# Turning q and the attention scores by transposing DMAs instead of on TensorE, in a fused attention and gated-FFN kernel

## The chip, the cores and the metric

The kernel runs on one core of one Trainium2 chip. The metric is the device time of one execution in microseconds (us). Executions of one kernel mostly agree within a few tenths of a per cent, so differences of 1% are readable with a handful of runs. The variants ran in several rounds, on different chips, each time with the kernel before beside them (medians 623.2 to 624.1 us): a ratio is within one round, a difference of two times from different rounds is good to about 1 us. The profiles are of single executions and give a span about 2 us shorter than the time of that execution.

## The reference, cut to what matters

Eight batches of 1024 tokens, eight heads of 64. Keys and values are first projected along the sequence from 1024 to 64 rows, so the scores are only 64 wide per head. The attention output, 8192 tokens by 512, goes through a gated feed-forward network (FFN).

```python
k_proj = np.einsum('ks,bhsd->bhkd', E, k)          # 64 x 64 per head
v_proj = np.einsum('ks,bhsd->bhkd', F, v)
scores = scale * np.matmul(q, k_proj.transpose(0, 1, 3, 2))
attn = softmax(scores)                             # over 64
attn_out = np.matmul(attn, v_proj)
# x: (8192, 512)
g = x @ w_gate                                     # 512 -> 1536
out = (g * sigmoid(g) * (x @ w_val)) @ w_out       # 1536 -> 512
```

The matmuls of this kernel contract over partitions. q arrives with tokens on partitions and must be turned so that the head dimension is there; the normalised scores must be turned once more before they meet the projected values.

## The kernel before: the parts that matter

Each batch is worked in eight steps j of 128 tokens, four to a half batch (ch). These are the two turns, both on TensorE, each with a copy from PSUM to SBUF:

```python
def u_T(b, j):                                     # turn q
    ps = ps_a.tile([P, NPAIR, P], BF16, name="qTp", tag="pa")
    src = qb[b, j // 4]
    for pr in range(NPAIR):                        # NPAIR = 4
        nc.tensor.transpose(out=ps[:, pr, :], in_=..., identity=ident_bf[:])
    t = aw.tile([P, NPAIR, P], BF16, name="qT", tag="qT")
    nc.scalar.copy(out=t[:], in_=ps[:])
    qT[b, j] = t

def u_A(b, j):                                     # turn the normalised scores
    ...                                            # four transposes into aTp
    nc.vector.tensor_copy(out=AT[b, ch][:, :, j % 4, :], in_=ps[:])
```

Between them stand `u_S` (score matmuls and the exponential on ACT), `u_R` (sum and reciprocal on DVE) and `u_N` (normalisation on POOL). `u_PV` multiplies the turned scores with the projected values and writes the FFN's input xT. `u_KV` projects k and v.

The FFN of one batch is 24 steps of 12 matmuls, and the attention of the next batch is dealt into its gaps, in 48 "slots" per batch, two to a step. The first half of batch 0 has no FFN to hide in and stands alone ahead of the loop:

```python
        load_k(0, 4); load_q(0, 0); load_v(0, 2)   # written on three lines
        ...                                        # weights, casts, load_q(0, 1)
        load_k(1)
        load_v(1)
        load_q(1, 0)
        load_q(1, 1)
        ...
        u_KV(0, 0, 8)
        u_KT(0)
        for n in range(7):                         # u_T, u_S, u_R, u_N, u_A of steps 0 to 3, pipelined
            ...
        for pr in range(NPAIR):
            u_PV(0, 0, pr)
```

The loads of k and v are issued from POOL and convert to bf16 on the way; the loads of q and the output stores are issued from SyncE (SP). Each of these two engines issues in program order: in the timeline before, SyncE's fourth q load goes out at 27.6 us, when its buffer is free, and nothing written after it goes out earlier.

The softmax here doesn't subtract the row's maximum and nothing guards it: scores larger than these inputs give would overflow.

Of the kernel before, what the change touches and what calls it, by code (L numbers as in the profile page):

```python
# [12 lines left out]
BF16 = mybir.dt.bfloat16  # L13
FP32 = mybir.dt.float32

B = 8
H = 8
S = 1024
D = 64
KP = 64  # L20
DM = H * D
DFF = 1536
P = 128
NJ = S // P
NPAIR = H // 2
NKT = DM // P
NFT = DFF // P
CH = 2
CW = 512
# [4 lines left out]
def kernel(  # L34
# [19 lines left out]
    nc = tc.nc  # L54
# [7 lines left out]
    aw = ctx.enter_context(tc.tile_pool(name="aw", bufs=2))  # L62
# [7 lines left out]
    ps_a = ctx.enter_context(tc.tile_pool(name="psa", bufs=3, space=bass.MemoryType.PSUM))  # L70

    ident_bf = const.tile([P, P], BF16, name="ident_bf")
# [4 lines left out]
    BD = [const.tile([P, NPAIR, P], BF16, name=f"BD{i}") for i in range(2)]  # L77
# [8 lines left out]
    kb, vb, qr, qb, xT, hT = {}, {}, {}, {}, {}, {}  # L86
# [85 lines left out]

    qT, ee, rr, AA, AT = {}, {}, {}, {}, {}

    def u_T(b, j):
        ps = ps_a.tile([P, NPAIR, P], BF16, name="qTp", tag="pa")
        src = qb[b, j // 4]
        for pr in range(NPAIR):
            nc.tensor.transpose(  # L179
                out=ps[:, pr, :], in_=src[:, j % 4, 2 * pr : 2 * pr + 2, :].rearrange('p h d -> p (h d)'), identity=ident_bf[:]  # L180
            )
        t = aw.tile([P, NPAIR, P], BF16, name="qT", tag="qT")
        nc.scalar.copy(out=t[:], in_=ps[:])  # L183
        qT[b, j] = t

    def u_S(b, j):
        ps = ps_a.tile([P, NPAIR, P], FP32, name="sc", tag="pa")
        t = qT.pop((b, j))
        for pr in range(NPAIR):
            nc.tensor.matmul(  # L190
                out=ps[:, pr, :], lhsT=t[:, pr, :], rhs=BD[b % 2][:, pr, :], start=True, stop=True
            )
        e = aw.tile([P, H, KP], FP32, name="ee", tag="ee", bufs=3)
        nc.scalar.activation(  # L194
            out=e[:].rearrange("p h k -> p (h k)"),
            in_=ps[:].rearrange("p a k -> p (a k)"),
            func=AF.Exp,
            scale=scale,
        )
        ee[b, j] = e  # L200

    def u_R(b, j):
        e = ee[b, j]
        z = aw.tile([P, H], FP32, name="zz", tag="zz", bufs=3)
        nc.vector.reduce_sum(out=z[:], in_=e[:], axis=AX.X)  # L205
        r = aw.tile([P, H], FP32, name="rr", tag="rr", bufs=3)
        nc.vector.reciprocal(out=r[:], in_=z[:])  # L207
        rr[b, j] = r

    def u_N(b, j):  # L210
        a = aw.tile([P, H, KP], BF16, name="AA", tag="AA", bufs=3)
        nc.gpsimd.tensor_tensor(  # L212
            out=a[:],
            in0=ee.pop((b, j))[:],
            in1=rr.pop((b, j))[:].unsqueeze(2).to_broadcast([P, H, KP]),
            op=ALU.mult,
        )
        AA[b, j] = a

    def u_A(b, j):  # L220
        ch = j // 4
        if (b, ch) not in AT:
            AT[b, ch] = aw.tile([P, NPAIR, 4, P], BF16, name="AT", tag="AT")
        ps = ps_a.tile([P, NPAIR, P], BF16, name="aTp", tag="pa")
        a = AA.pop((b, j))
        for pr in range(NPAIR):
            nc.tensor.transpose(  # L227
                out=ps[:, pr, :], in_=a[:, 2 * pr : 2 * pr + 2, :].rearrange('p h d -> p (h d)'), identity=ident_bf[:]
            )
        nc.vector.tensor_copy(out=AT[b, ch][:, :, j % 4, :], in_=ps[:])  # L230

    def u_PV(b, ch, pr):
        if (b, ch) not in xT:
            xT[b, ch] = x_pool.tile([P, NPAIR, CW], BF16, name="xT", tag=f"xT{ch}")
        ps = ps_a.tile([P, CW], FP32, name="pv", tag="pa")
        nc.tensor.matmul(  # L236
            out=ps[:],
            lhsT=BDV[b % 2][:, pr, :],
            rhs=AT[b, ch][:, pr].rearrange("p j t -> p (j t)"),
            start=True,  # L240
            stop=True,
        )
        nc.scalar.copy(out=xT[b, ch][:, pr, :], in_=ps[:])  # L243


    gp = {}
# [60 lines left out]
    slots = defaultdict(list)  # L307

    def put(s, fn, *a):
        slots[s].append((fn, a))  # L310

    def place(b):
        s0 = 48 * (b - 1)
        if b == 1:
            ks, tb, step = 28, 32, 2
        else:
            ks, tb, step = 0, 8, 5
        for i in range(4):
            put(s0 + ks + (i if b > 1 else i // 2), u_KV, b, i, 2)
        put(s0 + ks + (6 if b > 1 else 3), u_KT, b)  # L320
        for j in range(NJ):
            t = s0 + tb + step * j
            put(t, u_T, b, j)
            put(t + 2, u_S, b, j)
            put(t + 3, u_R, b, j)
            put(t + 3, u_N, b, j)
            put(t + 7, u_A, b, j)
        for ch in range(CH):
            if b == 1:
                at = (s0 + 48 - 2, s0 + 48 - 2, s0 + 48 - 1, s0 + 48 - 1) if ch == 0 else (  # L330
                    s0 + 57, s0 + 59, s0 + 62, s0 + 64)
            else:
                at = (36, 39, 41, 44) if ch == 0 else (57, 59, 62, 64)
                at = tuple(s0 + a for a in at)
            for pr in range(NPAIR):
                put(at[pr], u_PV, b, ch, pr)

    def run_slot(s):
        for fn, a in slots.pop(s, ()):
# [2 lines left out]
    with tc.manual_schedule():  # L342

        ef = []
        for which, src in (("E", E), ("F", F)):
            raw = const.tile([KP, S], FP32, name=f"{which}raw")
            nc.sync.dma_start(out=raw[:], in_=src)
            ef.append(raw)
        load_k(0, 4)
        load_q(0, 0)  # L350
        load_v(0, 2)
        for i in range(2):
            nc.vector.memset(BD[i][:], 0.0)
            nc.vector.memset(BDV[i][:], 0.0)
        load_w_gv(0)
        cast_q(0, 0)
        load_q(0, 1)
        load_w_gv(1)
        load_w_gv(2)
        load_wo(0)  # L360
        load_wo(1)
        cast_q(0, 1)
# [4 lines that stand above are left out]
        for which in range(2):  # L367
            for half in range(2):
                ps = ps_a.tile([P, 4, KP], FP32, name="efp", tag="pa")
                for i in range(4):  # L370
                    j = 4 * half + i
                    nc.tensor.transpose(
                        out=ps[:, i, :],
                        in_=ef[which][:, bass.ds(j, P, step=NJ)],
                        identity=ident_fp[:KP, :KP],
                    )
                js = slice(4 * half, 4 * half + 4)
                if which == 0:
                    nc.vector.tensor_copy(out=ET[:, js, :], in_=ps[:])
                else:  # L380
                    nc.scalar.copy(out=FT[:, js, :], in_=ps[:])

        u_KV(0, 0, 8)
        u_KT(0)
        for n in range(7):
            if n < 4:
                u_T(0, n)
            if 1 <= n < 5:
                u_S(0, n - 1)
                u_R(0, n - 1)  # L390
                u_N(0, n - 1)
            if n >= 3:
                u_A(0, n - 3)
        for pr in range(NPAIR):
            u_PV(0, 0, pr)
        for j in range(4, NJ):
            t = 3 * (j - 4)
            put(t, u_T, 0, j)
            put(t + 2, u_S, 0, j)
            put(t + 3, u_R, 0, j)  # L400
            put(t + 3, u_N, 0, j)
            put(t + 7, u_A, 0, j)
        for pr in range(NPAIR):
            put(19 + pr, u_PV, 0, 1, pr)
        for b in range(1, B):
            place(b)
        for b in range(2, B):
            s0 = 48 * (b - 2)
            put(s0 + 36, load_k, b)
            put(s0 + 40, load_v, b)  # L410
            put(s0 + 36, load_q, b, 0)
            put(s0 + 44, load_q, b, 1)
        for b in range(1, B):
            s0 = 48 * (b - 1)
            put(s0 + 1 if b > 1 else 27, cast_q, b, 0)
            put(s0 + 20 if b > 1 else 35, cast_q, b, 1)

        for s in slots:
            slots[s].sort(key=lambda x: x[0] not in (load_k, load_v, load_q, cast_q))

        for t in range(NIT):
            c, f = divmod(t, NFT)
            f_g(c, f)
            run_slot(2 * t)
            f_v(c, f)
            if c > 0:
                f_y(c - 1, f)
            run_slot(2 * t + 1)
        for f in range(NFT):
            f_y(B * CH - 1, f)  # L430
        assert not slots
# [30 lines left out]
```

## Time and profile before

| | before |
|---|---|
| time, median of 4 runs | 623.83 us |
| span of the profiled execution (it took 625.48 us) | 623.7 us |
| PE busy | 587.5 us (94%) |
| first gate matmul of the FFN (L252) | 41.67 us |
| steady batch | 72.2 us, PE busy for all of it |
| PE's waits for DMAs | 4.4 (E), 9.2 (first k), 8.7 (v: 8.1 first, 0.6 batch 2) |

The table has two messages. PE is full from 42 us on, so anything taken off PE there shortens the run by as much. Up to 42 us PE mostly waits, first for loads and then for a chain of small steps. The lines behind it are in the prediction below, with their reading.

```profile
out_dram<-ysb SPq DMA_DIRECT2D x1, 256.0 KB, 6.2
```

### The profile page before, as it was taken

What the parts mean: (1) busy time and instruction counts of PE and PEld (TensorE: products, weight loads), DVE (VectorE), ACT (ScalarE), POOL (GpSimd) and SP (SyncE); (2) the same over time, 40 slices, a digit from 0 to 9 for tenths busy, and PEclk for the clock granted to TensorE, in tenths of its full rate; (3) what the DMA queues carried; (4) which work ended last, traced back from release to release, by engine and by line L of the source; (5) the groups of instructions that cost most, each with busy time, mean ns of one, the idle gap of its engine ahead of it and who ended that gap; (6) DMA issues with size and microseconds to landing.
All of it is one profiled execution on the core that took longest, in us unless ns stands there. A gap on an engine that the chain in (4) does not pass through costs nothing.

```text
span 623.7 us, 8720 instructions
## 1 busy us (share of the span) xinstructions
PE 587.5 (94%) x3312; PEld 283.3 (45%) x3312; DVE 352.2 (56%) x614; ACT 258.9 (42%) x459; POOL 126.6 (20%) x164
## 2 busy tenths in 40 slices
PE   1369999999999999999999999999999999999996
PEld 1135455445544455444544545445553455444442
DVE  1049566566655665556655566555665666655540
ACT  1145446254444445344452544344353444433321
POOL 4634013221220311203220212202112121100000
PEclk9959999999999999999999999999999999999999
DMA  9999049000770019200490008600192000000001
GB/s 194 244 229 205 6 114 222 20 35 18 148 190 23 29 34 221 101 34 35 70 251 35 35 35 159 162 34 18 44 243 85 18 35 35 34 35 33 36 34 68
DMA packets 47498, 56.14 MB, mean 90 GB/s; under 512 B 1760, under 2 KB 39136, under 8 KB 47456
## 3 DMA queue, kind: packets, MB, share of 16 engines
q0 software_dynamic: 21440, 21.50, 21.9%
q1 hardware_dynamic: 26016, 34.08, 16.0%
q8 instruction: 26, 0.43, 0.3%
q14 instruction: 16, 0.13, 0.1%
HBM read 60.29 MB, written 16.78 MB: 124 GB/s over the span
## 4 chain that ended last, share of the span: by engine, by line
PE 91%; DMA 5%; POOL 1%; ACT 1%; DVE 1%; issue 0%; ACTq 0%; POOLq 0%; DVEq 0%
PE vps L267 26%; PE gps L252 26%; PE yps L290 26%; DMA vb<-in_v_dram 5%; PE kvp L145 3%; PE pv L236 2%; PE aTp L227 2%; PE sc L190 2%; PE qTp L179 2%; POOL AA L212 0%; ACT ysb L299 0%; POOL kb L93 0%; PE kTp L165 0%; DVE zz L205 0%; ACT ee L194 0%
## 5 line engine op out<-in xcount | busy, mean ns | idle before, releaser
L276 DVE SCALAR_TENSOR_TENSOR s<-th,gps 128x512 f32<-128x512 f32 x192 | 130.8, 681 | 134.9 <-ACT th L260 133.8
L252 PE MATMUL gps<-xT,wg 128*128 128x512 bf16 x768 | 198.4, 380 | 0.2
L290 PE MATMUL yps<-wo,hT 128*128 128x512 bf16 x768 | 195.8, 379 | 2.8 <-ACT ysb L299 2.8
L267 PE MATMUL vps<-xT,wv 128*128 128x512 bf16 x768 | 197.7, 380 | 0.0
L260 ACT ACTIVATE th<-gps 128x512 f32<-128x512 f32 x192 | 114.7, 597 | 170.2 <-PE gps L252 146.8
L212 POOL TENSOR_TENSOR AA<-ee,rr 128x512 bf16<-128x512 f32 x64 | 66.6, 1042 | 400.9 <-DVE rr L207 283.3
L281 DVE TENSOR_TENSOR hT<-s,vps 128x512 bf16<-128x512 f32 x192 | 132.0, 688 | 25.3 <-PE vps L267 6.9
L290 PEld LDWEIGHTS <-hT 128*128 128x128 bf16 x768 | 75.1, 98 | 94.1 <-issue 4.0
L252 PEld LDWEIGHTS <-wg 128*128 128x128 bf16 x768 | 71.7, 98 | 79.7 <-issue 6.9
L267 PEld LDWEIGHTS <-wv 128*128 128x128 bf16 x768 | 71.2, 98 | 78.1 <-issue 6.7
L299 ACT ACTIVATE ysb<-yps 128x512 f32<-128x512 f32 x64 | 38.2, 597 | 73.6 <-PE yps L290 73.6
L194 ACT ACTIVATE ee<-sc 128x512 f32<-128x512 f32 x64 | 38.2, 597 | 31.1 <-PE sc L190 30.8
L205 DVE TENSOR_REDUCE zz<-ee 128x8 f32<-128x512 f32 x64 | 43.6, 682 | 13.1 <-ACT ee L194 13.0
L183 ACT COPY qT<-qTp 128x512 bf16<-128x512 bf16 x64 | 37.4, 584 | 25.8 <-PE qTp L179 25.8
L230 DVE COPY AT<-aTp 128x512 bf16<-128x512 bf16 x64 | 26.9, 421 | 34.1 <-PE aTp L227 33.4
L243 ACT CAST xT<-pv 128x512 bf16<-128x512 f32 x64 | 36.8, 584 | 19.2 <-PE pv L236 19.2
L120 POOL CAST qb<-qr 128x512 bf16<-128x512 f32 x64 | 36.5, 612 | 8.1 <-DMA qr<-in_q_dram 8.1
L227 PE MATMUL aTp<-ident_bf,AA 128*128 128x128 bf16 x256 | 25.6, 224 | 4.4 <-POOL AA L212 4.4
L145 PE MATMUL kvp<-kb,ET 128*64 128x512 bf16 x64 | 20.9, 421 | 9.2 <-DMA kb<-in_k_dram 9.2
L227 PEld LDWEIGHTS <-AA 128*128 128x128 bf16 x256 | 19.8, 100 | 19.6 <-POOL AA L212 5.4
L145 PE MATMUL kvp<-vb,FT 128*64 128x512 bf16 x64 | 20.4, 418 | 8.7 <-DMA vb<-in_v_dram 8.7
L179 PE MATMUL qTp<-ident_bf,qb 128*128 128x128 bf16 x256 | 25.2, 222 | 0.6 <-DVE BDV L159 0.4
(37 smaller groups left out, 170.2 us busy)
## 6 DMA issues: line engine op xcount, KB each, us to landing
qr<-in_q_dram SPq DMA_DIRECT2D x16, 1024.0 KB, 12.6
out_dram<-ysb SPq DMA_DIRECT2D x64, 256.0 KB, 2.0
kb<-in_k_dram POOLq DMA_DIRECT2D x7, 1024.0 KB, 11.4
vb<-in_v_dram POOLq DMA_DIRECT2D x7, 1024.0 KB, 14.4
wg<-in_moe_w_gate_dram POOLq DMA_DIRECT2D x3, 512.0 KB, 22.2
wv<-in_moe_w_val_dram POOLq DMA_DIRECT2D x3, 512.0 KB, 25.7
wo<-in_moe_w_out_dram POOLq DMA_DIRECT2D x2, 768.0 KB, 29.1
kb<-in_k_dram POOLq DMA_DIRECT2D x4, 256.0 KB, 9.4
```

What stands on the lines that cost most here:

```text
L145: nc.tensor.matmul(out=t[lo : lo + 64].rearrange("p h d -> p (h d)"), lhsT=w[:, j, :], rhs=src[:, :, j, :], start=(j == 0), stop=(j == NJ ...
L194: nc.scalar.activation(out=e[:].rearrange("p h k -> p (h k)"), in_=ps[:].rearrange("p a k -> p (a k)"), func=AF.Exp, scale=scale,)
L205: nc.vector.reduce_sum(out=z[:], in_=e[:], axis=AX.X)
L212: nc.gpsimd.tensor_tensor(out=a[:], in0=ee.pop((b, j))[:], in1=rr.pop((b, j))[:].unsqueeze(2).to_broadcast([P, H, KP]), op=ALU.mult,)
L227: nc.tensor.transpose(out=ps[:, pr, :], in_=a[:, 2 * pr : 2 * pr + 2, :].rearrange('p h d -> p (h d)'), identity=ident_bf[:])
L252: nc.tensor.matmul(out=ps[:], lhsT=wg[:, kt, f * P : (f + 1) * P], rhs=x[:, kt, :], start=(kt == 0), stop=(kt == NKT - 1),)
L260: nc.scalar.activation(out=th[:], in_=ps[:], func=AF.Tanh, scale=0.5)
L267: nc.tensor.matmul(out=ps[:], lhsT=wv[:, kt, f * P : (f + 1) * P], rhs=x[:, kt, :], start=(kt == 0), stop=(kt == NKT - 1),)
L276: nc.vector.scalar_tensor_tensor(out=s1[:], in0=th[:], scalar=1.0, in1=g[:], op0=ALU.add, op1=ALU.mult)
L281: nc.vector.tensor_tensor(out=hT[c][:, f, :], in0=s1[:], in1=ps[:], op=ALU.mult)
L290: nc.tensor.matmul(out=yy[c][:], lhsT=hT[c][:, f, i * P : (i + 1) * P], rhs=wo[:, f, :], start=(f == 0), stop=(f == NFT - 1),)
L299: nc.scalar.activation(out=ysb[:], in_=yy.pop(c)[:], func=AF.Copy, scale=0.5)
```

## The change

The intent: 512 TensorE transposes and 128 copies from PSUM go, and 32 DMAs of 512 KB each turn the data between SBUF tiles, beside everything else. The core of the diff:

```diff
-    def u_T(b, j):
-        ...                                        # 4 transposes, 1 ACT copy
+    def u_T(b, ch):
+        t = aw.tile([P, 4 * NPAIR, P], BF16, name="qT", tag="qT")
+        nc.sync.dma_start_transpose(
+            out=t[:], in_=qb[b, ch][:].rearrange("p j h d -> p (j h d)")
+        )
+        qT[b, ch] = t
...
-    def u_A(b, j):
-        ...                                        # 4 transposes, 1 DVE copy
+    def u_A(b, ch):
+        t = aw.tile([P, 4, NPAIR, P], BF16, name="AT", tag="AT")
+        nc.sync.dma_start_transpose(
+            out=t[:].rearrange("p j a t -> p (j a) t"),
+            in_=AA.pop((b, ch))[:].rearrange("p j h d -> p (j h d)"),
+        )
+        AT[b, ch] = t
...
     def place(b):
         s0 = 48 * (b - 1)
+        sj = (4, 6, 8, 10, 14, 16, 18, 20)         # slots of u_S
+        sp = (26, 28, 30, 32, 36, 38, 40, 42)      # slots of u_PV
+        kv, tq, ta = 0, (1, 10), (13, 23)          # u_KV, u_T, u_A
+        ...                                        # other numbers for b == 1
-        for i in range(4):
-            put(s0 + ks + (i if b > 1 else i // 2), u_KV, b, i, 2)
+        put(s0 + kv, u_KV, b, 0, 8)                # all 16 projections in one slot
...                                                # start of batch 0
+        u_T(0, 0)
+        for n in range(4):
+            u_S(0, n); u_R(0, n); u_N(0, n)        # written on three lines
+        u_A(0, 0)
...
-            put(s0 + 36, load_q, b, 0)
-            put(s0 + 44, load_q, b, 1)
+            put(s0 + 30, load_q, b, 0)
+            put(s0 + 38, load_q, b, 1)
```

Besides the transposes it does three more things: it gathers the k and v projections of a batch in one slot, it re-deals the slots, and it loads and casts q earlier.

More of the change, by code (lines that the diff above doesn't have):

```diff
@@ L173 @@
     qT, ee, rr, AA, AT = {}, {}, {}, {}, {}
-    def u_T(b, j):
-        ps = ps_a.tile([P, NPAIR, P], BF16, name="qTp", tag="pa")
-        src = qb[b, j // 4]
-        for pr in range(NPAIR):
-            nc.tensor.transpose(
-                out=ps[:, pr, :], in_=src[:, j % 4, 2 * pr : 2 * pr + 2, :].rearrange('p h d -> p (h d)'), identity=ident_bf[:]
-            )
-        t = aw.tile([P, NPAIR, P], BF16, name="qT", tag="qT")
-        nc.scalar.copy(out=t[:], in_=ps[:])
-        qT[b, j] = t
+    def u_T(b, ch):
[4 more added lines that the diff above has]
+        qT[b, ch] = t
     def u_S(b, j):
         ps = ps_a.tile([P, NPAIR, P], FP32, name="sc", tag="pa")
-        t = qT.pop((b, j))
+        t = qT[b, j // 4]
         for pr in range(NPAIR):
             nc.tensor.matmul(
-                out=ps[:, pr, :], lhsT=t[:, pr, :], rhs=BD[b % 2][:, pr, :], start=True, stop=True
+                out=ps[:, pr, :],
+                lhsT=t[:, 4 * (j % 4) + pr, :],
+                rhs=BD[b % 2][:, pr, :],
+                start=True,
+                stop=True,
             )
@@ L210, in u_N @@
     def u_N(b, j):
-        a = aw.tile([P, H, KP], BF16, name="AA", tag="AA", bufs=3)
+        if j % 4 == 0:
+            AA[b, j // 4] = aw.tile([P, 4, H, KP], BF16, name="AA", tag="AA")
         nc.gpsimd.tensor_tensor(
-            out=a[:],
+            out=AA[b, j // 4][:, j % 4],
             in0=ee.pop((b, j))[:],
@@ L217, in u_N @@
         )
-        AA[b, j] = a
-    def u_A(b, j):
-        ch = j // 4
-        if (b, ch) not in AT:
-            AT[b, ch] = aw.tile([P, NPAIR, 4, P], BF16, name="AT", tag="AT")
-        ps = ps_a.tile([P, NPAIR, P], BF16, name="aTp", tag="pa")
-        a = AA.pop((b, j))
-        for pr in range(NPAIR):
-            nc.tensor.transpose(
-                out=ps[:, pr, :], in_=a[:, 2 * pr : 2 * pr + 2, :].rearrange('p h d -> p (h d)'), identity=ident_bf[:]
-            )
-        nc.vector.tensor_copy(out=AT[b, ch][:, :, j % 4, :], in_=ps[:])
+    def u_A(b, ch):
[5 more added lines that the diff above has]
+        AT[b, ch] = t
     def u_PV(b, ch, pr):
@@ L234, in u_PV @@
             xT[b, ch] = x_pool.tile([P, NPAIR, CW], BF16, name="xT", tag=f"xT{ch}")
-        ps = ps_a.tile([P, CW], FP32, name="pv", tag="pa")
+        ps = ps_a.tile([P, 4, P], FP32, name="pv", tag="pa")
         nc.tensor.matmul(
@@ L238, in u_PV @@
             lhsT=BDV[b % 2][:, pr, :],
-            rhs=AT[b, ch][:, pr].rearrange("p j t -> p (j t)"),
+            rhs=AT[b, ch][:, :, pr, :],
             start=True,
@@ L242, in u_PV @@
         )
-        nc.scalar.copy(out=xT[b, ch][:, pr, :], in_=ps[:])
+        nc.scalar.copy(out=xT[b, ch][:, pr, :], in_=ps[:].rearrange("p j t -> p (j t)"))
     gp = {}
@@ L313, in place @@
         s0 = 48 * (b - 1)
+        sj = (4, 6, 8, 10, 14, 16, 18, 20)
+        sp = (26, 28, 30, 32, 36, 38, 40, 42)
+        kv, tq, ta = 0, (1, 10), (13, 23)
         if b == 1:
-            ks, tb, step = 28, 32, 2
-        else:
-            ks, tb, step = 0, 8, 5
-        for i in range(4):
-            put(s0 + ks + (i if b > 1 else i // 2), u_KV, b, i, 2)
-        put(s0 + ks + (6 if b > 1 else 3), u_KT, b)
-        for j in range(NJ):
-            t = s0 + tb + step * j
-            put(t, u_T, b, j)
-            put(t + 2, u_S, b, j)
-            put(t + 3, u_R, b, j)
-            put(t + 3, u_N, b, j)
-            put(t + 7, u_A, b, j)
-        for ch in range(CH):
-            if b == 1:
-                at = (s0 + 48 - 2, s0 + 48 - 2, s0 + 48 - 1, s0 + 48 - 1) if ch == 0 else (
-                    s0 + 57, s0 + 59, s0 + 62, s0 + 64)
-            else:
-                at = (36, 39, 41, 44) if ch == 0 else (57, 59, 62, 64)
-                at = tuple(s0 + a for a in at)
+            kv, tq, ta = 24, (25, 30), (34, 42)
+            sj = (28, 29, 30, 31, 36, 37, 38, 39)
+            sp = (44, 45, 46, 47, 52, 54, 56, 58)
+        put(s0 + kv, u_KV, b, 0, 8)
+        put(s0 + kv + 2, u_KT, b)
+        for ch in range(CH):
+            put(s0 + tq[ch], u_T, b, ch)
+        for j in range(NJ):
+            put(s0 + sj[j], u_S, b, j)
+            put(s0 + sj[j] + 1, u_R, b, j)
+            put(s0 + sj[j] + 1, u_N, b, j)
+        for ch in range(CH):
+            put(s0 + ta[ch], u_A, b, ch)
             for pr in range(NPAIR):
-                put(at[pr], u_PV, b, ch, pr)
+                put(s0 + sp[4 * ch + pr], u_PV, b, ch, pr)
     def run_slot(s):
@@ L384 @@
         u_KT(0)
-        for n in range(7):
-            if n < 4:
-                u_T(0, n)
-            if 1 <= n < 5:
-                u_S(0, n - 1)
-                u_R(0, n - 1)
-                u_N(0, n - 1)
-            if n >= 3:
-                u_A(0, n - 3)
+        u_T(0, 0)
+        for n in range(4):
+            u_S(0, n)
+            u_R(0, n)
+            u_N(0, n)
+        u_A(0, 0)
         for pr in range(NPAIR):
             u_PV(0, 0, pr)
+        put(0, u_T, 0, 1)
         for j in range(4, NJ):
-            t = 3 * (j - 4)
-            put(t, u_T, 0, j)
-            put(t + 2, u_S, 0, j)
-            put(t + 3, u_R, 0, j)
-            put(t + 3, u_N, 0, j)
-            put(t + 7, u_A, 0, j)
+            t = 6 + j - 4
+            put(t, u_S, 0, j)
+            put(t + 1, u_R, 0, j)
+            put(t + 1, u_N, 0, j)
+        put(11, u_A, 0, 1)
         for pr in range(NPAIR):
@@ L410 @@
             put(s0 + 40, load_v, b)
-            put(s0 + 36, load_q, b, 0)
-            put(s0 + 44, load_q, b, 1)
+            put(s0 + 30, load_q, b, 0)
+            put(s0 + 38, load_q, b, 1)
         for b in range(1, B):
             s0 = 48 * (b - 1)
-            put(s0 + 1 if b > 1 else 27, cast_q, b, 0)
-            put(s0 + 20 if b > 1 else 35, cast_q, b, 1)
+            put(s0 - 6 if b > 1 else 20, cast_q, b, 0)
+            put(s0 + 4 if b > 1 else 26, cast_q, b, 1)
         for s in slots:
-            slots[s].sort(key=lambda x: x[0] not in (load_k, load_v, load_q, cast_q))
+            slots[s].sort(key=lambda x: x[0] not in (load_k, load_v, load_q, cast_q, u_T))
         for t in range(NIT):
```

## The prediction

> **What bounds the kernel now.** I read the page of the kernel before first: its busy shares and its forty slices. TensorE (PE) is busy 94% of the span, the other engines 56% or less, and what PE lacks is all at the start.
>
> ```profile
> PE 587.5 (94%) x3312; PEld 283.3 (45%) x3312; DVE 352.2 (56%) x614; ACT 258.9 (42%) x459; POOL 126.6 (20%) x164
> ...
> PE   1369999999999999999999999999999999999996
> ...
> DMA  9999049000770019200490008600192000000001
> ```
>
> Each digit is a fortieth, 15.6 us, so PE waits in the first three (47 us), where the DMA engines are at nine tenths, and is full afterwards. Then the chain that ended last, by line:
>
> ```profile
> PE vps L267 26%; PE gps L252 26%; PE yps L290 26%; DMA vb<-in_v_dram 5%; PE kvp L145 3%; PE pv L236 2%; PE aTp L227 2%; PE sc L190 2%; PE qTp L179 2%; POOL AA L212 0%; ACT ysb L299 0%; POOL kb L93 0%; PE kTp L165 0%; DVE zz L205 0%; ACT ee L194 0%
> ```
>
> The two transposes, aTp and qTp, are on the chain, 2.2% and 2.0% in the finer listing, 26 us. Busy time can't be used for this (a pipelined transpose shows 222 ns), so I read starts in PE's order of time:
>
> ```profile
> 92.22 0.39 PE L227 MATMUL aTp<-ident_bf,AA 128*128 128x128 bf16 x4
> 92.45 1.03 PE L252 MATMUL gps<-xT,wg 128*128 128x512 bf16 x4
> ```
>
> Four transposes hold PE from 92.22 to 92.45, about 0.225 us; four 512-column matmuls take 0.86. The stretches show whether PE has slack once it is running (first column pair: length and PE busy):
>
> ```profile
> 110.00:182.00 72.00, 72.00 (x418) 35.13 (x416) 44.65 (x79) 31.36 (x56) 15.02 (x19) 1.00 0.35 84
> 327.00:399.60 72.60, 72.60 (x417) 34.79 (x414) 43.80 (x76) 32.56 (x58) 14.97 (x20) 1.00 0.36 88
> ```
>
> None: a batch takes 72.2 us and PE is busy for all of it at full clock; VectorE (44 us) has much. So after the start **PE time is the run time**. The start is another stage, read from the timeline of all engines:
>
> ```profile
> 1.99 25.99 SPq L111 DMA_DIRECT2D qr<-in_q_dram  x4
> ...
> 28.74 0.40 PE L179 MATMUL qTp<-ident_bf,qb 128*128 128x128 bf16 x4
> ...
> 33.78 3.05 POOL L212 TENSOR_TENSOR AA<-ee,rr 128x512 bf16<-128x512 f32 x3
> ...
> 40.01 1.87 PE L236 MATMUL pv<-AT,BDV 128*128 128x512 bf16 x4 [0.52 <-DVE AT L230]
> ...
> 41.67 1.91 PE L252 MATMUL gps<-xT,wg 128*128 128x512 bf16 x4
> ```
>
> The first half of batch 0 goes through attention alone, 28.7 to 41.7, and nothing else can run on PE in that time. SyncE (SPq) issues the fourth load of q only by 28 us, because that load waits for the cast of the second. The listing of DMA issues for that moment gives its landing, and the stretches give the end of the initial pile of loads (last columns: clock, DMA share, GB/s):
>
> ```profile
> qr<-in_q_dram SPq DMA_DIRECT2D x1, 1024.0 KB, 13.3
> ```
> ```profile
> 60.00:62.00 2.00, 2.00 (x14) 1.01 (x12) 1.89 (x4) 0.60 (x1) 2.00 (x4) 1.00 1.22 207
> 62.00:64.00 2.00, 2.00 (x11) 0.90 (x10) 1.57 (x4) 1.06 (x2) 1.73 (x4) 1.00 0.38 65
> ```
>
> That load lands at about 27.6 + 13.3 = 41 us, and the DMA engines are saturated until about 62 us.
>
> **What the Trainium skill says.** "TensorE: Matmul & The Clock Gate", section Back-to-back issue gap: N/2.4 + 2.5 ns for N columns. Four of 128 give 0.223 us, as the trace (0.225). "VectorE: DVE Perf Modes", section The three transpose paths, puts a 128x128 bf16 transpose at 390 ns on TensorE and 1309 ns on the DMA crossbar. "DMA: Bandwidth & Descriptors", section Latency and other measured facts, gives transposing DMAs 261 GB/s in one kernel. The same page, section Queues, rings and completion order, says that on each DMA engine the descriptors of a queue are consumed in ring order. The trace of before holds no transposing DMA, so the last three are untested; that the four q loads pile up on one queue is seen.
>
> **The change, part by part.**
>
> Removed: per 128 tokens four transposes of q and four of the scores with one ACT copy (584 ns) and one DVE copy (421 ns). There are 64 such steps, 128 groups of four. Eight groups lie in the start (first half of batch 0); the other 120 lie where PE has no slack: 120 x 0.225 = **27 us less**. The copies give ACT 37 us and DVE 27 us back, which is worth nothing in time, as neither is the bound.
>
> Added: 32 transposing DMAs, 128x2048 bf16 (512 KB) each, on SyncE's queue. Their duration D is the open number. From the skill: 512 KB at 261 GB/s is 2.0 us; with the same 2.0 us that the trace shows as the whole latency of a 256 KB store as a floor for the ends, about 4 us. Sixteen blocks one after another at 1309 ns would be 21 us. I take 5.5 us alone (estimate, nearer to the first as blocks should overlap) and 7.5 to 8 while the initial loads saturate the engines.
>
> In the steady state, what lies between a transposing DMA and its reader? SyncE issues in program order, so the first q transpose of a batch goes out after the store of the batch before (slot -1), its cast being long done. Scores start in slot 4: seven groups of 0.86 us, the 16 k/v projection matmuls now in one slot (16 x 0.216 = 3.5), the k transposes, minus about 1 us for ACT and SyncE: some 8.7 us. The second q transpose has about 12 us, those of the scores about 14 slots of 1.4 us, 20 us. At D = 5.5 all of it is hidden.
>
> In the start, nothing is hidden. The first q transpose is issued at 28 us, but behind the fourth q load on the same queue: it can begin at about 41 us, where before the TensorE transposes began at 28.7. Then the chain: 41 + D1; scores, exponential, sum and reciprocal (0.3 + 0.6 + 0.7 + 0.2, with hand-overs 2.0) and four normalisations on POOL at 1.04, together 6.2 us; D2 for the score transpose; PV and its evacuation 2.0. The first gate matmul starts at 49.2 + D1 + D2 = 49.2 + 8 + 7.5 = 64.7 us instead of 41.7: **23 us more**. In the first twelve FFN steps (two slots of about 0.94 us each) the last score transpose of batch 0 has some 6 us until PV in slot 19: 0.5 us of wait, say.
>
> Moved: the q loads and casts earlier, the k/v projection into one slot; no cost that I see. The v load of batch 2 is just in time in the kernel before (a wait of 0.64 us); the same again.
>
> Sum: 623.9 - 27 + 23 + 0.5 = 620.4, say **621 us**. Most of the gain of the whole run is given back in the start.
>
> **The rivals.**
>
> 1. Gain without the price: the transposes slip past the loads or take 3.5 us. For it: the skill's bandwidth figures, and the loads in the way are only 1 MB. The start would then cost 49.2 + 7 - 41.7 = 14.5 us or less, and the time would be 611 or below. Against it: the fourth load of q is ahead on the same queue whatever D is.
> 2. DMA latency becomes the bound in the steady state too. For it: the 1309 ns of a single block. With D = 10 the first q transpose comes 1.3 us late in six or seven batches (9 us), the start costs some 30 us, and the second half of batch 0 waits 5 to 7: about 643 us. With D = 12, above 660.
> 3. The store queue: SyncE stands in a transposing DMA that waits for POOL's normalisation, so output stores go late and hold ysb. Against: three buffers at one store per 8.6 us leave 17 us or more. Under 1 us.
> 4. Another engine becomes the bound after PE falls to 68.8 us a batch. Against: DVE falls from 44 to 40 us. Nothing.
>
> **Range and chances.** Everything hangs on D, once in the steady state (free up to about 8.7 us) and twice in the start. D from 3 to 10 us gives 608 to 643; with some room for what the saturated engines do to small descriptors: 606 to 650. Faster by over 2% (under 611.4) needs D1 + D2 below 7 us: 0.18. Slower by over 2% (over 636.3) needs D of about 9 us or more alone, or a contended D1 of 15 us: 0.26. Within 2%: 0.56.
>
> **What would show it.** A steady batch of 68.8 us (3.4 less) with PE full: the removal right. The first gate matmul at about 65 us: the start right; at 56 or earlier, rival 1. The first q transpose landing at about 49, well after it was issued: the queueing right. A latency of 4 to 8 us per transposing DMA late in the run: D right. PE waiting at the score matmuls for qT in every batch: rival 2. The prediction is wrong above all if a transposing DMA is far slower than 5.5 us, or if the wait in the start is shorter because queue order doesn't hold it back.

## More of the kernel before

The wait for the v load of batch 2:

```profile
109.75 0.38 PE L145 MATMUL kvp<-vb,FT 128*64 128x512 bf16 x1 [0.64 <-DMA vb<-in_v_dram]
```

## The result

| | before | after |
|---|---|---|
| time, median of 4 runs | 623.83 us | 640.44 us |
| ratio | | 1.0263 (1.0245 to 1.028) |
| span, profiled | 623.7 us | 638.5 us |
| PE busy | 587.5 us | 555.3 us |
| first gate matmul | 41.67 us | 70.76 us |

The result is correct, and the kernel is 2.6% slower: inside the predicted range, outside what was thought likeliest.

The page of the changed kernel, the rows for PE and DMA and the chain that ended last:

```profile
PE 555.3 (87%) x2800; PEld 256.8 (40%) x2800; DVE 326.9 (51%) x550; ACT 223.1 (35%) x395; POOL 126.9 (20%) x164
...
PE   1201699959998999899999999999999999999995
...
DMA  9999532992288244932295427924493232000101
...
PE 68%; DMA 25%; DVE 2%; POOL 2%; ACT 1%; issue 1%; SPq 0%; DVEq 0%; POOLq 0%; ACTq 0%
```

PE lost 32 us of work, as intended. But the hole at the start has grown from three slices to five, there are a 5 and two 8s in slices that were full, and a quarter of the chain is now DMA, where it was 5%. The waits of PE name the places (us in total, times, longest):

```profile
PE sc L186 <- DMA qT<-qb: 25.1, 1, 25.1
...
PE pv L232 <- DMA AT<-AA: 20.3, 7, 13.4
...
PE kvp L145 <- DMA vb<-in_v_dram: 15.7, 2, 8.1
```

The first line and the 13.4 of the second are the start. What is left of the second, 20.3 - 13.4 = 6.9 us, is six short waits for a score transpose in the running part: five of 0.7 to 1.7 us at the second halves of batches 2 to 6, and one of 0.4 at the first half of batch 1. Of the third, 8.1 is the first v, as before, and 7.6 is new. The timeline of the start (start, length, engine, line):

```profile
27.69 15.20 SPq L177 DMA_TRANSPOSE qT<-qb  x1
...
53.77 1.89 PE L186 MATMUL sc<-BD,qT 128*128 128x128 bf16 x16 [25.13 <-DMA qT<-qb]
...
60.20 1.32 SPq L222 DMA_TRANSPOSE AT<-AA  x1
...
69.08 1.89 PE L232 MATMUL pv<-AT,BDV 128*128 128x512 bf16 x4 [13.42 <-DMA AT<-AA]
...
70.76 1.91 PE L248 MATMUL gps<-xT,wg 128*128 128x512 bf16 x4
```

The first transposing DMA is issued at 27.7 us, its reader runs at 53.8. The second takes from 60.2 to 69.0. The FFN starts 29 us later than before.

The new wait for v lies at batch 2, and it costs twice, because the clock has fallen when v arrives:

```profile
133.15 0.40 PE L145 MATMUL kvp<-kb,ET 128*64 128x512 bf16 x1
141.12 0.58 PE L145 MATMUL kvp<-vb,FT 128*64 128x512 bf16 x1 [7.57 <-DMA vb<-in_v_dram]
141.12 0.63 PE L145 MATMUL kvp<-kb,ET 128*64 128x512 bf16 x1
141.50 0.63 PE L145 MATMUL kvp<-vb,FT 128*64 128x512 bf16 x1
```

The projection pairs start 0.42 us apart there; in a later batch the sixteen take 1.85 us on the chain instead of 3.56, so 1.7 us more are lost. The granted clock is 0.50 from 141 to 144 us and 1.00 again from 145; over 110 to 182 us that makes 0.95.

Last, the durations. The first answer is the listing of issues for a stretch of batch 3 with no load in it, the second for a stretch 15 us later (size and time from issue to landing):

```profile
AT<-AA SPq DMA_TRANSPOSE x1, 4.2
```
```profile
kb<-in_k_dram POOLq DMA_DIRECT2D x1, 1024.0 KB, 11.1
vb<-in_v_dram POOLq DMA_DIRECT2D x1, 1024.0 KB, 17.7
out_dram<-ysb SPq DMA_DIRECT2D x1, 256.0 KB, 6.6
AT<-AA SPq DMA_TRANSPOSE x1, 17.7
```

**The same transfer takes 4.2 us alone and 17.7 us beside the k and v loads.** An output store, 2.0 us alone, takes 6.6 us there too. That much the kernel before showed already: twelve of its stores run beside loads of k, v and q, and eleven of them took 5.6 to 7.6 us (one is the store of 6.2 us shown above, beside a k or v load; 2.0 us is the median of all 64 stores). So the record held a measured slowdown of about three times beside loads before anything was changed, and the prediction used only the 2.0. This is the reading from which the theory follows.

### The profile page after: what moved, and what is told of

Its sections match the earlier page's. It is cut to its first block, busy times and chain, and to the rows that moved or that the text cites. A ratio compares the mean times of both kernels' runs of the same rounds, so it can differ in the third digit from the quotient of the medians. Undisturbed runs are those within 1.5% of the kernel's fastest.

```text
span 638.5 us, 7629 instructions
## 1 busy us (share of the span) xinstructions
PE 555.3 (87%) x2800; PEld 256.8 (40%) x2800; DVE 326.9 (51%) x550; ACT 223.1 (35%) x395; POOL 126.9 (20%) x164
## 2 busy tenths in 40 slices
DMA packets 114054, 72.85 MB, mean 114 GB/s; under 512 B 68320, under 2 KB 105696, under 8 KB 114016
## 3 DMA queue, kind: packets, MB, share of 16 engines
q0 software_dynamic: 21440, 21.50, 21.8%
## 4 chain that ended last, share of the span: by engine, by line
PE 68%; DMA 25%; DVE 2%; POOL 2%; ACT 1%; issue 1%; SPq 0%; DVEq 0%; POOLq 0%; ACTq 0%
PE yps L286 21%; PE vps L263 21%; PE gps L248 20%; DMA AT<-AA 15%; DMA vb<-in_v_dram 6%; DMA qT<-qb 4%; PE kvp L145 2%; PE sc L186 2%; PE pv L232 2%; ACT ysb L295 1%; DVE zz L205 1%; POOL AA L213 1%; DVE s L272 0%; POOL kb L93 0%; DVE hT L277 0%
## 5 line engine op out<-in xcount | busy, mean ns | idle before, releaser
L248 PEld LDWEIGHTS <-wg 128*128 128x128 bf16 x768 | 75.1, 98 | 90.6 <-issue 2.1
L194 ACT ACTIVATE ee<-sc 128x512 f32<-128x512 f32 x64 | 37.8, 594 | 32.4 <-PE sc L186 27.7
L186 PE MATMUL sc<-BD,qT 128*128 128x128 bf16 x256 | 25.1, 225 | 25.1 <-DMA qT<-qb 25.1
L239 ACT CAST xT<-pv 128x512 bf16<-128x512 f32 x64 | 36.9, 582 | 19.6 <-PE pv L232 19.6
L232 PE MATMUL pv<-AT,BDV 128*128 128x512 bf16 x64 | 24.7, 395 | 20.3 <-DMA AT<-AA 20.3
L186 PEld LDWEIGHTS <-qT 128*128 128x128 bf16 x256 | 20.1, 101 | 39.4 <-DMA qT<-qb 25.3
L145 PE MATMUL kvp<-vb,FT 128*64 128x512 bf16 x64 | 18.6, 443 | 15.7 <-DMA vb<-in_v_dram 15.7
L158 DVE CAST BDV<-kvp 64x256 bf16<-64x256 f32 x8 | 3.4, 426 | 52.8 <-ACT ks L155 52.8
L145 PE MATMUL kvp<-kb,ET 128*64 128x512 bf16 x64 | 18.9, 441 | 8.4 <-DMA kb<-in_k_dram 8.4
L232 PEld LDWEIGHTS <-BDV 128*128 128x128 bf16 x64 | 6.3, 100 | 30.6 <-DMA AT<-AA 23.8
## 6 DMA issues: line engine op xcount, KB each, us to landing
qr<-in_q_dram SPq DMA_DIRECT2D x16, 1024.0 KB, 10.9
kb<-in_k_dram POOLq DMA_DIRECT2D x7, 1024.0 KB, 11.8
wg<-in_moe_w_gate_dram POOLq DMA_DIRECT2D x3, 512.0 KB, 21.8
```

The lines of the kernel that those rows point to most:

```text
L145: nc.tensor.matmul(out=t[lo : lo + 64].rearrange("p h d -> p (h d)"), lhsT=w[:, j, :], rhs=src[:, :, j, :], start=(j == 0), stop=(j == NJ ...
L186: nc.tensor.matmul(out=ps[:, pr, :], lhsT=t[:, 4 * (j % 4) + pr, :], rhs=BD[b % 2][:, pr, :], start=True, stop=True,)
L232: nc.tensor.matmul(out=ps[:], lhsT=BDV[b % 2][:, pr, :], rhs=AT[b, ch][:, :, pr, :], start=True, stop=True,)
L248: nc.tensor.matmul(out=ps[:], lhsT=wg[:, kt, f * P : (f + 1) * P], rhs=x[:, kt, :], start=(kt == 0), stop=(kt == NKT - 1),)
```

## The experiments

Theory: the removal on PE works as counted, but a transposing DMA is about four times slower while k, v or weights are being loaded. That is so during the whole start, and it holds up PE there, at batch 2 and at one place of each later batch. Rivals: the order of the queue on SyncE is what delays the transposes; or the loss is spread over the steady state; or other engines hold PE.

All variants start from the changed kernel, except where it is said.

### 1. Batch 0 back on TensorE

```diff
-        u_T(0, 0)
-        for n in range(4): ...
-        u_A(0, 0)
+        for n in range(7): ...                    # the start of the kernel before
```

The second half of batch 0 is turned on TensorE as well, in the slots of the kernel before.

> The changed kernel with batch 0 alone turned on TensorE again, as in the kernel before; batches 1 to 7 keep the transposing DMAs. Theory A (the start is the largest loss): the first gate matmul comes back from 71.0 us to about 41.7, so 29 us less, and the eight groups of four transposes that return beside the FFN cost 1.8 us: about 613 us. The waits for v in batch 2 (7.6 us) and for the score transposes of batches 2 to 7 (about 1.1 us each) stay. Rival B (the loss is spread over the steady state): 630 us or more.

Measured: 611.93 us (ratio to before 0.9806, 0.9792 to 0.9821), expected 613. The FFN starts at 42.15 us:

```profile
42.15 1.91 PE L271 MATMUL gps<-xT,wg 128*128 128x512 bf16 x4
```

So the start is the largest loss, 28.5 us of time, and with it undone the change gains 1.9% on the kernel before.

### 2. The q loads of batch 1 after the first two transposes

```diff
-        load_q(1, 0)
-        load_q(1, 1)
...
         u_A(0, 0)
+        load_q(1, 0)
+        load_q(1, 1)
```

> The changed kernel with the two q loads of batch 1 issued after the first two transposing DMAs instead of before them. Theory A (queue order: the first transposing DMA waited behind 2 MB of q loads on the same queue, and for the casts that those waited for): it is issued at about 18 us, lands at about 34 in place of 53.7, and the first gate matmul is at about 55 in place of 71: about 624 us. Rival B (only the share of the DMA engines that the k, v and weight loads leave it counts): its latency stays near 26 us, it lands at 44, the second takes longer too, and the first gate matmul is at 66 or later: 635 us or more.

Measured: 634.04 us (1.0157, 1.0129 to 1.0184), short of theory A's 624 and near rival B. The timeline shows why both are partly right:

```profile
17.49 8.72 SPq L177 DMA_TRANSPOSE qT<-qb  x1
...
36.91 1.89 PE L186 MATMUL sc<-BD,qT 128*128 128x128 bf16 x16 [8.96 <-DMA qT<-qb]
```
```profile
AT<-AA SPq DMA_TRANSPOSE x1, 17.8
```

The first transpose lands at 36.9 instead of 53.7: queue order did cost those 17 us. But the second one, issued at 43.3, now falls into the thick of the initial loads and takes 17.8 us, where in the changed kernel it ran at 60 to 69 us, when they were running out, and took 8.8. The FFN starts at 62.81, 8 us sooner, not 16. Moving a transposing DMA forward among the loads gives back half of what it gains.

### 3. No loads of k and v for batches 2 to 7 (wrong result)

```diff
-            put(s0 + 36, load_k, b)
-            put(s0 + 40, load_v, b)
+            kb[b], vb[b] = kb[b - 2], vb[b - 2]
```

> Wrong result on purpose: the changed kernel without the k and v loads of batches 2 to 7 (they use the tiles of batches 0 and 1 again). Theory A (a transposing DMA is four times slower beside the k and v loads): every score transpose of the second halves lands in 4.3 us in place of 17, the waits for them (6.9 us in all) and the wait for v in batch 2 with its cold clock (7.6 + 1.7 us) go: about 624 us. Rival B (the slow ones are slow because of what stands before them on SyncE's own queue, the output stores and q loads): they stay at 17 us and only the wait for v goes: 631 us.

Measured: 622.93 us (0.9978, 0.9961 to 0.9995), expected 624. The medians of all 16 score transposes, in the list of issues of the changed kernel and of this one:

```profile
AT<-AA SPq DMA_TRANSPOSE x16, 7.2
```
```profile
AT<-AA SPq DMA_TRANSPOSE x16, 4.4
```

PE waits for a score transpose once instead of seven times, at the start, and for v once (7.8):

```profile
PE pv L232 <- DMA AT<-AA: 13.5, 1, 13.5
```

The output stores and the q loads stand on SyncE's queue as before, so rival B falls: it is the loads from the other queue that make the transposes slow.

### 4. The k and v loads of batch 2 earlier

```diff
-            put(s0 + 36, load_k, b)
-            put(s0 + 40, load_v, b)
+            put(s0 + 36 if b > 2 else 26, load_k, b)
+            put(s0 + 40 if b > 2 else 28, load_v, b)
```

> The changed kernel with the k and v loads of batch 2 in slots 26 and 28 in place of 36 and 40. Theory A (POOL issues the v load of batch 2 only at 122 us, behind the normalisations, and TensorE waits for it): the wait of 7.6 us goes and so does the cold clock after it, 1.7 us: about 631 us. Rival B (TensorE would have waited there for something else, the score transpose of batch 1 or the projections): under 3 us of gain, 638 us.

Measured: 637.15 us (1.0204, 1.0184 to 1.0224), a gain of 3.3 where 9.3 was expected. The wait for v is gone, but another has come, in the order of time on PE:

```profile
108.01 0.61 PE L186 MATMUL sc<-BD,qT 128*128 128x128 bf16 x4 [4.38 <-DMA qT<-qb]
```

The loads now run beside the first q transpose of batch 1, which takes 19.3 us (88.6 to 108.0) instead of 4.6. The wait was moved, not removed: my expectation forgot to ask what the loads would meet at their new place.

### 5. PV of the second halves four slots later

```diff
-        sp = (26, 28, 30, 32, 36, 38, 40, 42)
+        sp = (26, 28, 30, 32, 40, 42, 44, 46)
```

> The changed kernel with the PV matmuls of the second halves of batches 2 to 7 four slots (5.6 us) later. Theory A (in the steady state only the second score transpose of a batch, 17 to 18 us beside the k and v loads, is late, by about 1.1 us): the six waits go, 6.9 us: 633 to 634 us, with the latencies unchanged at 17 us. Rival B (something else holds TensorE there and the wait moves): 638 us or more.

Measured: 633.34 us (1.0161, 1.0141 to 1.018), as expected. The transposes still take 17 to 18 us; nobody waits for them any more in batches 2 to 7. (That of batch 7 was never slow, 4.4 us: no load runs beside it.)

### 6. The kernel before, with the k and v projections gathered in one slot

```diff
-        for i in range(4):
-            put(s0 + ks + (i if b > 1 else i // 2), u_KV, b, i, 2)
+        put(s0 + ks, u_KV, b, 0, 8)
```

> The kernel before with one thing of the change alone: the sixteen k and v projection matmuls of a batch in one slot in place of four. Theory A (a part of the shorter steady batch, 67.7 us of TensorE work against 72.2, comes from this, as the removed transposes explain 3.6 of the 4.5 us): 0.9 us a batch in seven batches, about 618 us. Rival B (all of it comes from the transposes): 623 to 624 us.

Measured: 619.33 us (0.9938, 0.992 to 0.9955). The gathering alone gains 0.6%, some 4 us: less than my 6, but not nothing. A steady batch takes 71.5 us instead of 72.2. So part of the shorter steady batch had nothing to do with transposes.

### 7 and 8. Smaller packets in the k and v loads

Why are the transposes slow beside the loads? The changed kernel has 68,320 packets under 512 bytes, the kernel before 1,760: 2,080 for each transposing DMA, so about 128 of 256 bytes on each of 16 engines. The k and v loads of a batch are 2 MB in packets of 1 KB, also 128 on each engine. The mean load packet takes 104 ns (21.8% of 16 x 638.5 us over 21,440 packets), a transposing one some 33 (4.3 us over 128). If engines take the queues in turn, packet by packet, a transpose needs 128 x (33 + 104) = 17.5 us (an estimate from these numbers). To test it, the loads of batches 2 to 7 were cut so that each packet is half, then a quarter as large:

```diff
+    def load_half(t, src, b):
+        for i in range(2):                         # range(4), 2 and 128 for the quarter
+            nc.gpsimd.dma_start(
+                out=t[:, :, 4 * i : 4 * i + 4].rearrange("p h j d -> p h (j d)"),
+                in_=src[b].rearrange("h (p j) d -> p h (j d)", j=NJ)[:, :, 256 * i : 256 * i + 256],
+            )
```

> The changed kernel with the k and v loads of batches 2 to 7 cut so that each packet carries half the bytes (512 in place of 1024 in SBUF). Theory A (the transposing DMA has 128 packets of 256 bytes on each of the 16 engines and must give way to one load packet of 104 ns for each of them: 128 x (33 + 104) = 17.5 us): with packets of some 60 to 70 ns the score transpose beside them lands in about 12.5 us. Rival B (bytes are shared evenly, or the SBUF side is the limit): it stays at 17 us or gets slower.

> The changed kernel with each packet of the k and v loads of batches 2 to 7 a quarter as large (256 bytes in SBUF). Half packets brought the score transpose beside the loads from 17 to about 15 us. Theory A (turn for turn: it needs 128 turns on each engine, each as long as its own packet and one of the load): 9 to 12 us, well before the v load lands. Rival B (bytes are shared, or the SBUF side is the limit): 15 us or more.

Measured, one look each (632.71 and 636.43 us): the second score transposes of batches 2 to 6 took 14.3 to 15.9 us with half packets and 12.6 to 14.8 with quarter packets, against 16.8 to 17.9. One such transpose with half packets, then one with quarter packets:

```profile
AT<-AA SPq DMA_TRANSPOSE x1, 15.9
```
```profile
AT<-AA SPq DMA_TRANSPOSE x1, 13.4
```

The new load packets took 60 and 42 ns on average (the software queue's time less that of the 8,960 unchanged packets), so turn for turn would have given 12.0 and 9.6 us. The direction is theory A's: a transfer of more packets in all disturbs the transpose less. The size is about half.

The packets in the kept traces show why. In a transpose that runs alone the first packet moves 1.2 us after issue and the last 2.6 us later, so a packet's own turn is about 21 ns; the 33 had the latency in it, and that 17.5 met the 17.7 was chance. Beside loads the first packet moves only 4.7 to 5.3 us after issue, and the moving then takes 11.1 to 12.6 us; with half packets 8.9 to 10.5, with quarters 7.0 to 9.4. Turn for turn, with 21 ns, would be 16.0, 10.4 and 8.1: near for the cut packets, too long for the whole ones. The late first packet is not mainly the output store that SyncE issues 0.4 us earlier: with that store and no loads (experiment 3) it moves after 1.3 us, and with loads and nothing ahead on SyncE's queue (the second transpose of experiment 2) after 3.9. So both parts, the late start and the stretched moving, come with the loads. Why the first packet comes late and why 1 KB packets cost less than a full turn stays open. So does the time as a whole, which was shorter than the changed kernel's in both: cut loads land later, and with quarters PE waits four times for pieces of v.

### 9. A version that draws the consequences

Batch 0 on TensorE, q of batch 1 on TensorE, k and v of batch 2 loaded in slot 14, straight behind the initial loads and before any transposing DMA, and PV as in experiment 5:

```diff
+            if b == 1:
+                put(s0 + sj[j] - 2, u_Tp, b, j)    # q on TensorE
...
+            put(s0 + 36 if b > 2 else 14, load_k, b)
+            put(s0 + 40 if b > 2 else 14, load_v, b)
...
+        sp = (26, 28, 30, 32, 40, 42, 44, 46)
```

> A version meant to beat both: batch 0 turned on TensorE, q of batch 1 on TensorE, the k and v loads of batch 2 in slot 14, PV of the second halves later, all else by transposing DMAs. From the run with batch 0 on TensorE (611.9 us) the wait for v and its cold clock (9.3 us) go, eight groups of transposes return (1.8 us), and the waits for score transposes (5.6 us) go: about 599 us. If a wait only moves, as when the loads of batch 2 were moved alone, 605 us or more.

Measured: 594.74 us (0.9546, 0.9528 to 0.9564), correct, 4.5% faster than the kernel before. The stretch of one steady batch and more shows PE full again:

```profile
327.00:395.00 68.00, 68.00 (x350) 31.55 (x348) 40.81 (x69) 27.40 (x49) 14.65 (x18) 1.00 0.58 124
```

A steady batch takes 68.0 us (from the first projection of one batch, 309.56, to that of the next, 377.52).

### 10 and 11. One kind of transpose alone

Both have batch 0 on TensorE. In the one, only q of batches 1 to 7 is turned by DMA; in the other, only the scores. The other kind is done by TensorE in slots beside its neighbours:

```diff
-            put(s0 + ta[ch], u_A, b, ch)
+        for j in range(NJ):
+            put(s0 + sj[j] + 4, u_Ap, b, j)       # q only: scores on TensorE
```

> One part alone: batch 0 and all score transposes on TensorE, q of batches 1 to 7 by transposing DMA. Against the run with batch 0 on TensorE (611.9 us): 56 groups of four transposes return (12.6 us) and the waits for score transposes go (5.6 us): 619 us if the two parts simply add up; 625 us or more if the score transposes were the only part worth something.

> The other part alone: batch 0 and all q transposes on TensorE, scores of batches 1 to 7 by transposing DMA. Against the run with batch 0 on TensorE (611.9 us): 56 groups return (12.6 us), all waits stay: 624 us if the parts add up; less than 616 us if the q transposes by DMA cost what they save.

Measured: q only 605.61 us (0.9708, 0.9692 to 0.9724), scores only 622.5 us (0.9985, 0.9939 to 1.0031). Doing both, in experiment 1, took 611.93. So q alone is better than both: with the scores on TensorE no transposing DMA runs beside the v load of batch 2, which lands in 11.8 us, and no wait for it is in the list (at most 0.5 us: the sixteen projections take 2.32 us instead of 1.85). I had taken that wait as given and expected 619. As dealt here, the score transposes by DMA cost more than they save. Experiment 9 shows that this is a matter of where loads and readers are placed: there it is 10.9 us faster than q alone, and 56 groups of score transposes less, 8 of q more on PE count 10.8. The four runs of scores only lie between 619.2 and 626.68, so its loss against experiment 1 is clear, its size only roughly.

## Why the prediction was wrong

**PE bounds the run after the start, and 120 groups of four transposes are worth 27 us**: right. Without the waits a steady batch takes 68.0 us instead of 72.2. 3.6 of the 4.2 us are the transposes (16 groups of 0.225; the prediction's 3.4 a batch is a little short); the gathered projections, of which the prediction said only that they cost nothing, gave the rest, 0.7 us a batch and 4 us over the run in experiment 6.

**A transposing DMA takes 5.5 us alone**: right enough, 4.2 to 4.4. **"7.5 to 8 while the initial loads saturate the engines": this is the term that failed.** Beside the k and v loads it takes 17 to 18 us (experiment 3 takes the cause away, experiment 2 shows it inside the start), and the steady state was given no loaded duration at all. The sum for the start was 49.2 + D1 + D2 with D1 = 8 and D2 = 7.5. Measured from 41 us on, D1 was 12.8, and D2 8.8 only because the loads were ending. The start cost 29 us, not 23. Its form, the queueing behind the fourth q load and two exposed latencies, was right.

**"At D = 5.5 all of it is hidden"** in the steady state: wrong for the second score transpose of batches 2 to 6, for the same reason. I had given it 20 us of room and a duration of 5.5. The k and v loads are issued just beside it: POOL sends them as soon as its last normalisation ends, and the transpose waits for that too (in batch 3 it ends at 247.5 us; k goes out at 247.5, v at 248.4, the transpose, behind one store, at 248.9). The room was also less than counted, 16.2 us from issue to the time that PE wanted it. So at 17 to 18 us it was late by 0.7 to 1.7 us in five batches: with the 0.4 of batch 1 that is 6.9 us of waits, and about 7 us of time in experiment 5. The room of the first q transpose was smaller too, 7.1 us and not 8.7, since the sixteen projections take 1.85 us and not 16 x 0.216 = 3.5; at 4.4 us that did no harm.

**"The v load of batch 2 is just in time ...; the same again"**: wrong. Before, it was issued at 95.11, landed after 14.6 us and was wanted at 108.7, 13.6 us after issue. In the changed kernel POOL issued it at 122.17, it landed after 18.9 us beside a score transpose of 18.1, and PE wanted it after 11.2. Counted from the first gate matmul, PE got there 4.6 us sooner than before (62.4 instead of 67.0), POOL issued the load only 2.0 us sooner (51.4 instead of 53.4). So 4.3 us of the wait are the slower load and 2.6 the lost room, on top of the 0.6 that was there. That is a wait of 7.6 us, and 1.7 us of cold clock.

Taken together, to the 620.4 us of the prediction's sum: 6 for the start, 9 for v, 7 for the score transposes, less 4 for the gathered projections. That makes 638; 640.44 was measured. Of the 2 us left, 1.0 is two short waits of PE in the trace (0.7 at 85.6 us for VectorE, 0.3 at 132.8 for ScalarE); the rest is open.

That the time lies inside the range is in part luck. The range was worked out for one D of 3 to 10 us everywhere, with "some room" for the loads, and D alone was 4.4. The 22 us that were missing came from the neighbourhood of loads and from the v load, for which the sum had almost nothing, and the 4 us of the gathered projections, not foreseen either, hid part of it.

**The rivals**: the first (transposes slip past the loads) was refuted by the 25.1 us of wait at the start. The second (latency becomes the bound in the steady state) was right in kind, but it was put down to a long D everywhere and to the first q transpose of a batch; the true D is short and only grows beside loads, and what came late was the second score transpose. The third (output stores) and the fourth (another engine) did not appear in PE's waits. The chances hung on "D of about 9 us or more alone, or a contended D1 of 15 us"; the second condition is nearly what happened, and it had been given too little weight.

## What to carry to other kernels

When work moves from an engine to DMA, its duration is no longer a property of the transfer: ask which loads run beside it at each place, and take the duration from such a place. Where the trace has none of the new kind, look at what another transfer loses there: the stores' 2.0 and 6.2 us were such a warning. Before the main loop, where nothing hides latency and the loads are piled up, keep the work on the engine. In the loop, keep the loads away from the transfers that someone soon waits for, or give their reader more room; and after each step that shortens the loop check the loads that were just in time.

## What the Trainium skill lacked or had wrong

- "DMA: Bandwidth & Descriptors", section Latency and other measured facts, gives 261 GB/s for transposing DMAs in one kernel. Here 512 KB between SBUF tiles took 4.2 to 4.4 us from issue to landing when nothing else ran, some 122 GB/s with both ends counted; in the 2.6 us in which its packets moved it was some 200 GB/s.
- No page read here gives a figure for a transposing DMA beside loads. The runs show 16.8 to 18.1 us for the same 512 KB beside k and v loads from POOL's queue, four times as long, and a median of 4.4 when those loads are taken away. The packets, about 128 of 256 bytes on each engine, and the gain from smaller load packets (medians of 17.7, 15.4 and 13.5 us) fit in direction the turns between queues, packet by packet, that the section Queues, rings and completion order of the same page describes, but only about half of the effect; no run shows whether a packet of the trace is a packet of that page.
- "VectorE: DVE Perf Modes", section The three transpose paths, gives 1309 ns for a 128x128 block by DMA. Sixteen blocks in one DMA took 4.3 us, 270 ns each: its figure is not to be multiplied.
- "TensorE: Matmul & The Clock Gate", section Back-to-back issue gap: its formula for a single matmul held, 0.225 us measured for four transposes, 0.223 by the formula. Its figures for a stream of weight loads and matmuls, 81 ns at 128 columns and 131 ns at 512, did not: here it is 56 ns, and 215 ns (0.86 us for four).
